# A state-space scan and a low-rank mixer on one core: half a batch moved from plain to split products, and a new order

## The chip, the cores and the metric

The kernel runs on one core of a Trainium2 chip. A core has a matrix engine (PE, with PEld for its weight loads), a vector engine (DVE), a scalar engine (ACT), a general engine (POOL) and a queue engine (SP) that issues the DMAs. The metric is the time in microseconds on the device, from the start to the end of one execution; less is better.

## The reference

Two parts follow each other. The first is a scan over 768 positions for 4 batches and 8 heads (head size 32, state size 16), the second a mixer over the 256 channels that the heads make together.

```python
# scan, by chunks of 32 positions
L = np.exp(cum[:, :, :, None] - cum[:, :, None, :]) * causal
y_intra = ((Cc @ Bc^T) * L) @ xc
y_inter = (Cc @ state) * exp(cum)
state   = decay_full * state + sum(Bc x xc * decay_from_j)
# mixer on x = y laid out as (batch, position, 256)
h  = x^T @ U @ V                              # rank 32, along positions
u  = x + h^T
ch = np.maximum(u @ w_ch1, 0.0) @ w_ch2       # 256 -> 1024 -> 256
return u + ch
```

The weights U, V, w_ch1 and w_ch2 come as 64-bit floating point numbers and are turned into 32-bit ones on the core.

## The kernel before, in words

**An order written out by hand.** The whole program is a list of words, `PLAN`. The function `follow` reads it from left to right, and every word issues a small group of instructions. Each engine works off its own instructions in the order in which the words issued them, and waits for the data of the others. So the list sets the order on every engine, and a word that has to wait on one engine holds up what stands behind it on that engine alone.

**Loads**, all on SP's queue: `B k`, `X k` and `w n` bring the scan's B and C, its x, and a block of the weights. `k` counts pairs of 128-position chunks, 0 to 11, three for each batch. These loads are also held until the last DVE instruction issued before them is done. `YB`, `YX`, `YU` and `YV` are the same loads for B and C, x, U and V, without that hold. `YV` issues four DMAs of 48 KB, `YU` one of 192 KB, `YX` two of 128 KB, `YB` three.

**Weights.** `c n` appears three times for each block: the first time two DVE instructions and one of ACT, the second time one of DVE, the third time one of POOL. Block 0 is U and V together, so its first word needs the loads of both. Blocks 1 to 5 are the first layer, 6 to 9 the second. `R n` (two or three times) splits a weight block into halves of 12 bits for the one-pass products: an ACT copy, then a POOL subtraction and another ACT copy, then one DVE instruction. `v` spreads V over the partitions.

**Scan**, for pair k: `Q`, `P` scale B and C by decays (DVE); `V`, `T` turn them with PE and copy the result on ACT (and for some `V` on DVE); `g` forms the products of C and B (PE), `m` and `M` mask them (DVE), `s` the sums for the state (PE), `u` updates the state (DVE, then POOL), `i`, `n` and `j` make the output (PE; `j` waits for a small settling copy on DVE), and `y` copies it (ACT). `A` and `K` at the start make the decays. `t` and `O` turn the output back for the mixer.

**Mixer**, for batch b: `p`, `q` and `a` do the low-rank part (`a b.j` adds it to half j of the positions, 384 of them, on DVE). Then the two layers, for each half j. In the plain form a word `U b.j.m` makes one block of 128 hidden channels from 32-bit operands (two products) and a ReLU on ACT, and `d b.j.k.n`, n from 0 to 3, the second layer for 128 positions. In the split form `S b.j` first cuts u into a near part, a far part and a sum (one ACT instruction, two of DVE); for each block m, `f` makes four of six one-pass products and a scaling on ACT, `e` the last two and a ReLU on ACT, `h` the far part on DVE and, for odd m, the sum as well; `d b.j.k.n`, n from 0 to 5, is the second layer. The choice is in `down`:

```python
parts = b or j >= PLAIN
pieces = 6 if parts else 4
```

With `PLAIN = 2` both halves of batch 0 are plain, and the other three batches split.

**Buffers and fills.** Products go to eight banks of the accumulator memory, two under each of the tags w, x, z and y; a word that takes a bank waits until the last reader of that bank's earlier content is done. The tag `words` has 15 buffers for the weights' words, their temporaries, and the hidden channels. `F n` makes the next word that takes a bank run n idle blocks of 128 columns on PE ahead of its own products (line 136); `E n` runs n such blocks at once.

The lines that the profile names: L136 idle blocks, L202 the loads, L174 every DVE instruction (a helper issues them), L425 the last step of `c`, L439 the subtraction of `R`, L478 `V` and `T`, L510 `g`, L545 `s`, L630 `i`, L655 `n` and `j`, L682 `t` and `O`, L709 and L717 `p`, L727 `q`, L737 `a` and the closing product, L765 all products of the two layers, L858 `v`.

Of the kernel before, what the change touches and what calls it, by code (L numbers as in the profile page):

```python
# [13 lines left out]
FP32R = mybir.dt.float32r  # L14
WCOLS = 512
NWORDS = 15
PLAIN = 2
TAGS = {(2, 1): "yyy", (3, 0): "yyy", (3, 1): "yyy"}


# [11 lines left out]


PLAN = (
    'YB0 F2 A1 YB1 Q0.2 A0 Q0.0 Q0.1 YX0 K0 YB2 YV0 F5 V0.0.0 V0.1.1 F1 g0 Q1.2 Q1.1 s0 V1.1.2 YX1 '
    'Q1.0 V1.0.2 m0 M0 n0 YX2 F3 g1 Q2.0 Q2.2 u0 YU0 M1 Q2.1 i0 j0 y0 s1 F1 V2.0.2 m1 n1 w0 u1 '
    'V2.1.3 c0 c0 c0 E3 i1 g2 m2 YB3 w1 M2 E4 j1 y1 s2 B5 v0 O0.0 w4 u2 c2 t1 i2 P3 X3 c2 B4 w2 c2 '
    'n2 j2 T3 c1 c1 y2 T3 O2.1 X4 p0 P5 g3 m3 M3 q0 T5 T5 n3 a0.1 a0.0 B6 c1 s3 U0.1.0 P4 w3 U0.1.1 '
    'u3 T4 T4 U0.0.1 i3 c5 c5 c3 g4 X5 j3 c5 c3 w5 s4 U0.0.0 m4 R3 U0.1.6 c3 y3 U0.1.2 P6 U0.0.6 M4 '
    'T6 u4 T6 B7 i4 g5 c4 c4 n4 w6 s5 j4 y4 R1 M5 U0.0.7 c4 U0.1.3 m5 U0.1.7 U0.0.5 R3 c6 u5 U0.0.3 '  # L40
    'P7 T7 w8 n5 R0 i5 c7 R2 X6 c6 g6 w7 j5 c6 y5 T7 U0.1.5 t5 M6 U0.0.2 X9 B10 c7 t3 m6 R2 t4 R1 '
    'c8 U0.0.4 c8 p1 U0.1.4 c7 B8 q1 R4 X7 c8 d0.0.2.0 c9 d0.0.1.0 c9 d0.0.1.1 c9 d0.0.2.1 d0.0.2.2 '
    'd0.0.2.3 d0.1.0.0 a1.0 d0.1.0.1 P8 d0.1.0.2 S1.0 a1.1 R7 d0.0.1.2 d0.0.1.3 d0.1.0.3 s6 g7 m7 '
    'M7 n6 R0 f1.0.0 u6 R6 f1.0.1 f1.0.4 e1.0.0 h1.0.0 f1.0.5 e1.0.4 e1.0.1 f1.0.6 h1.0.4 i6 s7 j6 '
    'h1.0.1 d0.0.0.0 e1.0.5 R4 h1.0.5 f1.0.7 X8 e1.0.6 h1.0.6 d0.0.0.1 d0.0.0.2 e1.0.7 h1.0.7 '
    'f1.0.3 R5 f1.0.2 B9 u7 d0.1.1.0 X10 d0.0.0.3 P10 e1.0.2 R5 y6 h1.0.2 S1.1 e1.0.3 d0.1.2.0 '
    'd0.1.1.1 d0.1.1.2 h1.0.3 d0.1.2.1 d0.1.2.2 T8 T8 d0.1.2.3 d0.1.1.3 n7 s8 u8 i7 g8 j7 P9 s9 '
    'f1.1.0 m8 y7 R7 f1.1.1 d1.0.1.0 M8 e1.1.0 u9 d1.0.0.0 i8 n8 h1.1.0 s10 j8 d1.0.1.1 d1.0.1.2 R6 '
    'd1.0.1.3 R4 R5 u10 d1.0.0.1 d1.0.0.2 d1.0.1.4 e1.1.1 d1.0.0.3 R7 d1.0.2.0 R6 d1.0.2.1 d1.0.2.2 '
    'B11 d1.0.2.3 d1.0.0.4 d1.0.0.5 d1.0.1.5 d1.0.2.4 T10 h1.1.1 f1.1.6 f1.1.7 d1.0.2.5 e1.1.6 '  # L50
    'e1.1.7 f1.1.2 h1.1.6 h1.1.7 f1.1.3 f1.1.4 f1.1.5 X11 e1.1.2 e1.1.4 h1.1.2 h1.1.4 e1.1.3 h1.1.3 '
    'e1.1.5 P11 h1.1.5 T9 T9 d1.1.0.0 d1.1.0.1 d1.1.2.0 d1.1.2.1 d1.1.0.2 d1.1.2.2 d1.1.0.3 y8 t6 '
    'd1.1.2.3 d1.1.1.0 d1.1.1.1 d1.1.1.2 d1.1.1.3 d1.1.2.4 d1.1.0.4 d1.1.0.5 t7 d1.1.1.4 d1.1.1.5 '
    'd1.1.2.5 T10 t8 g9 p2 m9 M9 i9 g10 m10 q2 T11 T11 M10 n9 a2.0 s11 u11 j9 g11 i10 n10 y9 m11 '
    'S2.0 M11 t9 f2.0.0 f2.0.4 f2.0.1 e2.0.0 h2.0.0 e2.0.4 f2.0.5 e2.0.1 h2.0.4 h2.0.1 f2.0.6 '
    'e2.0.5 h2.0.5 f2.0.2 f2.0.3 j10 y10 e2.0.2 e2.0.3 f2.0.7 h2.0.2 h2.0.3 i11 n11 a2.1 e2.0.6 '
    'e2.0.7 j11 h2.0.6 d2.0.0.0 S2.1 y11 d2.0.1.0 d2.0.1.1 d2.0.0.1 f2.1.0 h2.0.7 d2.0.1.2 t11 t10 '
    'e2.1.0 h2.1.0 d2.0.1.3 d2.0.0.2 d2.0.0.3 f2.1.2 d2.0.1.4 d2.0.0.4 d2.0.0.5 d2.0.1.5 f2.1.3 '
    'd2.0.2.0 e2.1.2 h2.1.2 e2.1.3 d2.0.2.1 p3 d2.0.2.2 f2.1.1 f2.1.4 h2.1.3 d2.0.2.3 e2.1.1 f2.1.5 '
    'h2.1.1 e2.1.4 h2.1.4 d2.0.2.4 e2.1.5 q3 d2.0.2.5 h2.1.5 f2.1.6 f2.1.7 a3.0 e2.1.6 e2.1.7 '  # L60
    'h2.1.6 d2.1.2.0 d2.1.2.1 a3.1 d2.1.0.0 d2.1.0.1 d2.1.2.2 d2.1.0.2 S3.0 f3.0.3 f3.0.2 h2.1.7 '
    'd2.1.2.3 d2.1.0.3 f3.0.1 e3.0.2 h3.0.2 d2.1.0.4 e3.0.3 d2.1.0.5 h3.0.3 f3.0.0 e3.0.1 d2.1.1.0 '
    'd2.1.1.1 d2.1.1.2 e3.0.0 h3.0.0 f3.0.5 f3.0.4 d2.1.1.3 f3.0.6 e3.0.4 d2.1.2.4 e3.0.5 h3.0.1 '
    'f3.0.7 h3.0.4 d2.1.2.5 d2.1.1.4 e3.0.6 e3.0.7 d2.1.1.5 d3.0.2.0 d3.0.2.1 h3.0.6 d3.0.2.2 '
    'd3.0.0.0 d3.0.0.1 d3.0.0.2 S3.1 f3.1.0 f3.1.4 f3.1.5 h3.0.7 h3.0.5 d3.0.2.3 e3.1.0 f3.1.1 '
    'h3.1.0 d3.0.0.3 e3.1.4 f3.1.2 e3.1.5 d3.0.0.4 d3.0.0.5 d3.0.2.4 d3.0.2.5 d3.0.1.0 h3.1.4 '
    'd3.0.1.1 h3.1.5 e3.1.1 f3.1.6 f3.1.3 h3.1.1 d3.0.1.2 e3.1.2 e3.1.3 d3.0.1.3 h3.1.2 h3.1.3 '
    'f3.1.7 e3.1.6 h3.1.6 d3.0.1.4 d3.0.1.5 e3.1.7 d3.1.2.0 d3.1.2.1 h3.1.7 d3.1.2.2 d3.1.2.3 '
    'd3.1.1.0 d3.1.1.1 d3.1.2.4 d3.1.2.5 d3.1.1.2 d3.1.1.3 d3.1.0.0 d3.1.0.1 d3.1.0.2 d3.1.0.3 '
    'd3.1.1.4 d3.1.1.5 d3.1.0.4 d3.1.0.5 ')  # L70


@with_exitstack
def kernel(
# [624 lines left out]
    def mixer(b):  # L699
# [110 lines left out]
        def down(j, k, n):  # L810

            parts = b or j >= PLAIN
            pieces = 6 if parts else 4
# [141 lines left out]
```

## Time and profile before

| | |
|---|---|
| median of 3 runs | 227.23 us (226.65 to 227.78) |
| the profiled execution | 225.44 us, of which the span of instructions is 223.7 us |
| PE busy | 214.8 us, 96% of the span |
| DVE, ACT, POOL busy | 146.7, 107.9 and 33.8 us |
| granted PE clock | 0.999 |
| DMA | 14.59 MB, queue busy 32.3% of the span, nearly all before 70 us |
| chain that ended last | PE 88%, SP's queue 5%, DVE 3% |

Times in the rows are microseconds from the start of the span. A product's duration in a row is how long that one was under way; products overlap, so what a step costs is read from the chain of work or from where the next one starts. A plain product of 32-bit operands shows as two records.

### The profile page before, as it was taken

The numbers are of one execution on the slowest core, as the hardware profiler recorded it, in microseconds if no ns is written. First come the engines' busy times: TensorE is split into PE (matmuls) and PEld (weight loads), VectorE is DVE, ScalarE is ACT, GpSimd is POOL, SyncE is SP. The second block draws the span as 40 slices with busy tenths as digits, with TensorE's granted clock in tenths as the row PEclk, the third lists the DMA queues.
The fourth block names the chain that finished last, engine by engine and source line by source line (L and its number), as shares of the span: only waits on it lengthen the run. The fifth ranks groups of instructions, "written<-read, shape, count | busy, mean of one in ns | idle before, by whom it ended". The sixth has DMA issues, their size and how long they took to land.

```text
span 223.7 us, 7032 instructions
## 1 busy us (share of the span) xinstructions
PE 214.8 (96%) x3024; PEld 182.1 (81%) x3024; DVE 146.7 (66%) x311; ACT 107.9 (48%) x250; POOL 33.8 (15%) x43
## 2 busy tenths in 40 slices
PE   7878999999999999999999999999999999999994
PEld 4645655666668888887999997797999999999993
DVE  4867779927853866759636737978825966484821
ACT  3334746575781354461425624577336555554510
POOL 3012301642834020223400000000000000000000
PEclk9999999999999999999999999999999999999999
DMA  6968889962973010461032301000010000101011
GB/s 81 142 105 151 172 134 175 231 139 84 196 97 52 26 50 0 61 107 50 7 47 70 50 22 53 3 3 3 0 50 0 25 3 23 38 8 50 1 50 47
DMA packets 69520, 14.59 MB, mean 65 GB/s; under 512 B 63792, under 2 KB 67696, under 8 KB 69488
## 3 DMA queue, kind: packets, MB, share of 16 engines
q1 hardware_dynamic: 69488, 14.13, 32.3%
q8 instruction: 24, 0.39, 0.8%
q14 instruction: 8, 0.07, 0.1%
HBM read 10.98 MB, written 3.15 MB: 63 GB/s over the span
## 4 chain that ended last, share of the span: by engine, by line
PE 88%; SPq 5%; DVE 3%; DMA 1%; issue 1%; ACT 1%
PE x L765 31%; PE z L765 23%; PE y L765 12%; SPq L202 5%; PE y L655 3%; PE y L630 3%; PE w L682 2%; PE x L510 2%; PE w L545 2%; DMA x<-in_x_dram 1%; PE w L478 1%; DVE M L174 1%; PE z L510 1%; PE w L709 1%; PE x L737 1%; PE w L136 1%
## 5 line engine op out<-in xcount | busy, mean ns | idle before, releaser
L765 PE MATMUL x<-u,w 128*128 128x384 f32 x144 | 32.8, 344 | 0.2 <-DVE M L174 0.2
L765 PE MATMUL z<-u,w 128*128 128x384 f32 x144 | 32.6, 342 | 0.0
L174 DVE SCALAR_TENSOR_TENSOR words<-words 128x768 fp32r<-128x768 f32 (+3 forms) x34 | 30.1, 887 | 1.6
L770 ACT ACTIVATE x<-x 128x384 f32<-128x384 f32 (+1 forms) x30 | 13.6, 454 | 28.4 <-PE x L765 28.4
L765 PEld LDWEIGHTS z<-u,w 128*128 128x128 f32 x144 | 24.9, 188 | 0.6 <-DVE M L174 0.2
L765 PEld LDWEIGHTS x<-u,w 128*128 128x128 f32 x144 | 24.4, 188 | 1.0 <-issue 0.3
L765 PE MATMUL x<-w2c,words 128*128 128x256 f32 x112 | 22.9, 341 | 0.0
L174 DVE SCALAR_TENSOR_TENSOR words<-x,words 128x384 fp32r<-128x384 f32 x24 | 13.1, 554 | 14.8 <-ACT words L799 12.9
L572 POOL TENSOR_TENSOR Sm<-S,own 128x256 f32<-128x256 f32 (+1 forms) x12 | 8.1, 676 | 84.9 <-DVE S L174 47.5
L765 PEld LDWEIGHTS x<-w2c,words 128*128 128x128 f32 x112 | 18.2, 189 | 1.6
L765 PE MATMUL y<-w,words 128*128 128x256 f32 x144 | 19.3, 282 | 0.0
L770 ACT ACTIVATE z<-z 128x384 f32<-128x384 f32 (+1 forms) x27 | 12.5, 465 | 13.0 <-PE z L765 12.6
L765 PEld LDWEIGHTS y<-w,words 128*128 128x128 f32 x144 | 18.7, 190 | 0.0
L174 DVE SCALAR_TENSOR_TENSOR words<-z,words 128x384 fp32r<-128x384 f32 x24 | 13.2, 551 | 5.4 <-ACT words L799 5.4
L799 ACT ACTIVATE words<-z 128x384 fp32r<-128x384 f32 x24 | 11.7, 492 | 9.9 <-PE z L765 9.7
L799 ACT ACTIVATE words<-x 128x384 fp32r<-128x384 f32 x24 | 11.6, 491 | 7.8 <-PE x L765 7.8
L765 PE MATMUL x<-w,words 128*128 128x256 f32 x96 | 13.8, 286 | 0.0
L174 DVE SCALAR_TENSOR_TENSOR S<-S,kept,w 128x64 f32<-128x64 f32 x40 | 11.2, 279 | 2.8 <-PE w L545 1.2
L174 DVE TENSOR_TENSOR ytok<-x,ytok 128x256 f32<-128x256 f32 x10 | 4.2, 423 | 13.2 <-PE x L765 13.2
L655 PE MATMUL y<-M,x 64*32 64x64 f32 x768 | 12.0, 223 | 0.9 <-DVE settled L174 0.9
L765 PEld LDWEIGHTS x<-w,words 128*128 128x128 f32 x96 | 12.5, 190 | 0.3 <-issue 0.2
L655 PEld LDWEIGHTS y<-M,x 64*32 64x32 f32 x768 | 7.8, 105 | 5.8 <-DVE settled L174 1.9
(150 smaller groups left out, 409.7 us busy)
## 6 DMA issues: line engine op xcount, KB each, us to landing
words<-in_moe_w_ch_dram SPq DMA_DIRECT2D x7, 512.0 KB, 4.9
x<-in_x_dram SPq DMA_DIRECT2D x24, 128.0 KB, 3.5
out_dram<-ytok SPq DMA_DIRECT2D x24, 128.0 KB, 1.7
bc<-in_B_dram SPq DMA_DIRECT2D x24, 64.0 KB, 2.9
bc<-in_C_dram SPq DMA_DIRECT2D x12, 128.0 KB, 3.1
words<-in_moe_w_ch_dram SPq DMA_DIRECT2D x2, 256.0 KB, 3.8
words<-in_moe_V_dram SPq DMA_DIRECT2D x4, 48.0 KB, 3.4
words<-in_moe_U_dram SPq DMA_DIRECT2D x1, 192.0 KB, 3.4
```

The costliest lines, as they stand in the source:

```text
L136: nc.tensor.matmul(out=t[:, :m * P].rearrange("p (m i) -> p m i", i=P), lhsT=ident, rhs=ident[:, None, :].to_broadcast([P, m, P]), start=T ...
L174: self.last = call(*args, **kwargs)
L202: op = issuer[0].dma_start(**kwargs)
L510: nc.tensor.matmul(out=g[r][cols, c], lhsT=s["T"][rows, 0, c, cols], rhs=s["Cm"][rows, :, :, ts(2 * c + p, Q)].rearrange("r v t i -> r v i ...
L545: nc.tensor.matmul(out=s["A"][p][ts(r, Q), v], lhsT=s["BC"][half, 0, v, 2 * r:2 * r + 2].rearrange("p h n -> p (h n)"), rhs=x_sb[k][half, ...
L572: nc.gpsimd.tensor_tensor(out=s["Sm"][:, sl], in0=s["S"][:, sl].rearrange("p i (s d) -> p i s d", s=2), in1=own2[:, b, 4 * q + sl.start:4 ...
L630: behind["first"].append(nc.tensor.matmul(out=y[r // 2][ts(r % 2, H), c, p], lhsT=own[ts(r, Q)], rhs=s["T"][ts(r, Q), 1, :, ts(2 * c + p, ...
L655: product = nc.tensor.matmul(out=y[n][ts(i, Q), c, p], lhsT=x_sb[k][half, c, h], rhs=s["M"][half, h // 2, c, h % 2], start=fresh(k, n, [i] ...
L682: nc.tensor.transpose(out=t[:, c, g], in_=yT[b][:, g, ts(2 * q + c, P)], identity=ident)
L765: nc.tensor.matmul(out=t, lhsT=lhsT, rhs=rhs, start=start, stop=True, skip_group_check=True)
L770: nc.scalar.activation(t, t, AF.Copy, scale=1.0 + EPS)
L799: nc.scalar.activation(gs[j, m // 2][0][:, m % 2], t, AF.Relu, scale=NEAR)
```

## The change

`PLAIN` becomes 1: the first half of batch 0 stays plain, the second half takes the split form. The eight words `U0.1.m` go; `S0.1`, eight each of `f0.1.m`, `e0.1.m` and `h0.1.m`, and six more words `d0.1.k.n` come. The whole list stands in a new order. The words `F` are placed anew (6, 5, 4, 3 and 4 blocks in place of 2, 5, 1, 3 and 1), and the two words `E3` and `E4` go. No function changes. The two lists as far as the second layer of batch 0 (from batch 2 on they are much alike):

```diff
@@ -14,7 +14,7 @@
 FP32R = mybir.dt.float32r
 WCOLS = 512
 NWORDS = 15
-PLAIN = 2
+PLAIN = 1
 TAGS = {(2, 1): "yyy", (3, 0): "yyy", (3, 1): "yyy"}
...
 PLAN = (
-    'YB0 F2 A1 YB1 Q0.2 A0 Q0.0 Q0.1 YX0 K0 YB2 YV0 F5 V0.0.0 V0.1.1 F1 g0 Q1.2 Q1.1 s0 V1.1.2 YX1 '
-    'Q1.0 V1.0.2 m0 M0 n0 YX2 F3 g1 Q2.0 Q2.2 u0 YU0 M1 Q2.1 i0 j0 y0 s1 F1 V2.0.2 m1 n1 w0 u1 '
-    'V2.1.3 c0 c0 c0 E3 i1 g2 m2 YB3 w1 M2 E4 j1 y1 s2 B5 v0 O0.0 w4 u2 c2 t1 i2 P3 X3 c2 B4 w2 c2 '
-    'n2 j2 T3 c1 c1 y2 T3 O2.1 X4 p0 P5 g3 m3 M3 q0 T5 T5 n3 a0.1 a0.0 B6 c1 s3 U0.1.0 P4 w3 U0.1.1 '
-    'u3 T4 T4 U0.0.1 i3 c5 c5 c3 g4 X5 j3 c5 c3 w5 s4 U0.0.0 m4 R3 U0.1.6 c3 y3 U0.1.2 P6 U0.0.6 M4 '
-    'T6 u4 T6 B7 i4 g5 c4 c4 n4 w6 s5 j4 y4 R1 M5 U0.0.7 c4 U0.1.3 m5 U0.1.7 U0.0.5 R3 c6 u5 U0.0.3 '
-    'P7 T7 w8 n5 R0 i5 c7 R2 X6 c6 g6 w7 j5 c6 y5 T7 U0.1.5 t5 M6 U0.0.2 X9 B10 c7 t3 m6 R2 t4 R1 '
-    'c8 U0.0.4 c8 p1 U0.1.4 c7 B8 q1 R4 X7 c8 d0.0.2.0 c9 d0.0.1.0 c9 d0.0.1.1 c9 d0.0.2.1 d0.0.2.2 '
-    'd0.0.2.3 d0.1.0.0 a1.0 d0.1.0.1 P8 d0.1.0.2 S1.0 a1.1 R7 d0.0.1.2 d0.0.1.3 d0.1.0.3 s6 g7 m7 '
-    'M7 n6 R0 f1.0.0 u6 R6 f1.0.1 f1.0.4 e1.0.0 h1.0.0 f1.0.5 e1.0.4 e1.0.1 f1.0.6 h1.0.4 i6 s7 j6 '
-    'h1.0.1 d0.0.0.0 e1.0.5 R4 h1.0.5 f1.0.7 X8 e1.0.6 h1.0.6 d0.0.0.1 d0.0.0.2 e1.0.7 h1.0.7 '
-    'f1.0.3 R5 f1.0.2 B9 u7 d0.1.1.0 X10 d0.0.0.3 P10 e1.0.2 R5 y6 h1.0.2 S1.1 e1.0.3 d0.1.2.0 '
-    'd0.1.1.1 d0.1.1.2 h1.0.3 d0.1.2.1 d0.1.2.2 T8 T8 d0.1.2.3 d0.1.1.3 n7 s8 u8 i7 g8 j7 P9 s9 '
...
+    'F6 A1 YB1 YB0 A0 Q0.0 YX0 Q1.2 Q0.2 Q0.1 V0.0.0 YX1 YU0 V0.1.1 YB2 K0 YV0 w2 Q1.0 F5 g0 s0 YX2 '
+    'u0 Q1.1 s1 m0 M0 YB3 V1.0.2 F4 V1.1.2 c0 c0 n0 Q2.2 i0 g1 j0 y0 F3 w1 Q2.0 B5 Q2.1 V2.0.2 u1 '
+    'm1 M1 c3 O0.0 s2 c3 V2.1.3 i1 w3 n1 j1 u2 c0 y1 g2 w0 c3 X3 B4 P3 T3 m2 w4 c2 i2 T3 w7 t1 M2 '
+    'n2 j2 P5 y2 T5 w8 c4 X4 O2.1 T5 p0 c4 g3 M3 m3 q0 w6 F4 c4 X5 v0 P4 c1 s3 n3 u3 R2 a0.0 a0.1 '
+    'T4 T4 c5 U0.0.2 U0.0.3 i3 c8 c2 c1 g4 j3 s4 y3 U0.0.4 m4 M4 c8 c2 B6 c9 U0.0.1 c5 c1 R0 c5 '
+    'U0.0.0 n4 u4 c7 c8 w5 s5 i4 g5 u5 j4 B10 y4 P6 B7 T6 T6 U0.0.7 M5 m5 n5 R0 c9 i5 t3 j5 c9 X7 '
+    'y5 c6 c6 R1 c6 U0.0.6 t5 t4 R3 X6 c7 c7 g6 p1 M6 m6 P7 U0.0.5 R4 q1 d0.0.2.0 d0.0.2.1 B8 T7 R1 '
+    'R5 a1.0 R3 R7 T7 S0.1 X8 d0.0.1.0 d0.0.1.1 d0.0.2.2 d0.0.2.3 R2 d0.0.1.2 n6 R4 s6 u6 R6 '
+    'd0.0.1.3 s7 g7 m7 R6 i6 B9 f0.1.2 f0.1.0 M7 f0.1.1 e0.1.2 h0.1.2 e0.1.0 h0.1.0 f0.1.3 P8 '
+    'e0.1.1 f0.1.4 R5 d0.0.0.0 h0.1.1 e0.1.3 e0.1.4 h0.1.4 R7 f0.1.5 d0.0.0.1 X10 d0.0.0.2 h0.1.3 '
+    'u7 f0.1.6 d0.0.0.3 R7 R6 e0.1.5 h0.1.5 f0.1.7 j6 s8 e0.1.7 e0.1.6 d0.1.1.0 R5 d0.1.0.0 '
+    'd0.1.0.1 d0.1.1.1 d0.1.1.2 d0.1.2.0 h0.1.6 d0.1.2.1 y6 d0.1.0.2 h0.1.7 d0.1.0.3 u8 R4 d0.1.1.3 '
+    'd0.1.2.2 d0.1.2.3 d0.1.0.4 d0.1.0.5 S1.0 T8 P9 X9 d0.1.2.4 d0.1.1.4 d0.1.2.5 d0.1.1.5 f1.0.6 '
...
```

## The prediction

> **What bounds the kernel now.** I read the busy time of the engines by stretch first.
>
> ```profile
> 0.00:25.00 25.00, 20.75 (x490) 13.36 (x490) 16.58 (x57) 10.21 (x31) 5.17 (x17) 1.00 0.78 123
> 25.00:50.00 25.00, 24.59 (x516) 15.60 (x509) 18.69 (x47) 15.30 (x37) 8.04 (x8) 1.00 0.87 175
> 50.00:75.00 25.00, 24.81 (x233) 17.77 (x232) 15.84 (x30) 14.55 (x32) 10.96 (x9) 1.00 0.54 102
> 200.00:224.00 24.00, 20.51 (x157) 20.25 (x155) 10.30 (x18) 7.78 (x19) 0.00 (x0) 0.98 0.10 34
> ```
>
> Columns: stretch, length, busy us of PE, PEld, DVE, ACT, POOL, granted clock, DMA share, GB/s. PE is full from 25 on. Only the first 25 us (which hold idle blocks as well) and the tail have room. So the end is the moment at which the unbroken PE work begins, plus the work then left. Next, the chain that ended last (start, us, what, records), for the prices:
>
> ```profile
> 40.02 5.36 PE x L765 x16
> 68.79 3.57 PE x L765 x17
> 122.98 0.70 PE x L765 x4
> 193.60 3.46 PE y L765 x29
> ```
>
> First row: four steps U0 (plain products, four records each), 1.34 us a step. Second: one 128-row group of the plain second layer, 16 records and a closing one: 3.57. Third: one step f, 0.70, or 0.175 a record; step e has two records, 0.35. Fourth: 0.119 a record of the one-pass second layer, so 25 records (24 and a closing one) take 2.98. Last, the order of time in the front:
>
> ```profile
> 9.10 1.98 SPq L202 DMA_DIRECT2D words<-in_moe_V_dram  x4
> 18.96 0.63 DVE L174 TENSOR_SCALAR words<-words 128x384 f32<-128x384 f32 x2 [0.30 <-DMA words<-in_moe_U_dram]
> 27.68 1.54 PE L709 MATMUL w<-ytok,UV 128*32 128x256 f32 x12
> 33.21 1.56 PE L765 MATMUL x<-yT,w1f 128*128 128x384 f32 x4
> ```
>
> V's four loads are issued at 9.10 to 11.08. The first conversion (c0, which needs U and V both) starts the moment that U has landed. p0 is at 27.68. The first large product, U0.1.0, is at 33.21: there the dense work begins, and 223.7 - 33.2 = 190.5 us follow.
>
> **PE work removed.** Eight steps U0.1 at 1.34 become f and e at 1.05: 2.3 less. Three groups d0.1 go from 3.57 to 2.98: 1.8 less. Together 4.1. On a full engine this counts whole, wherever it stands.
>
> **DVE and ACT work added.** DVE: split 2 x 0.957, eight h at 0.553, four joins at 0.958: 10.2 us. ACT: 0.85, eight scalings at 0.476, three at 0.37: 5.8 us. Both stand behind f0.1, where PE has some 20 us of f, e and d, so I cost them at nothing: from f0.1.2 to the last d0.1 the list holds 22 us of PE beside 17 to 19.5 of DVE (with and without the 0.08 by which neighbours overlap), and in the old list's like stretch, 75 to 110, DVE had 24.9 of 35 and PE lost 0.4. If that cover failed, the price is at most the 4.4 of the eight h. The twelve words buffers that they take are free, since every c word stands ahead of f0.1.
>
> **Fills.** 19 blocks of 128 columns become 22. The chain's "18.01 0.66 PE w L136 x2" is the three blocks of E3: 0.22 us a block. They cost only where PE was not going to wait.
>
> **The front, which is reordered.** The likely end hangs on when U0.0.2, the new first large product, can start. I walk there with durations of the rows. (a) Six fills ahead of A1, from 3.6 on, let A1 start at 4.9, not 4.74; ACT's second F ends near 6.45, the four BC pieces at 7.7, V0.0.0 and V0.1.1 at 8.05. In SP's queue YB0 now stands behind YB1, and at that place loads landed in time. (b) K0 occupies PE to 8.9, then five fills to 10.0. g0 could have begun near 9.3 (T of V0.1.1), so F5 costs 0.7. g0 ends 10.7, s0 11.2. u0 now stands ahead of the masks on DVE: 12.5, then Q1.1, m0 and M0: 14.2, where M0 ended at 11.38 before. (c) Next on DVE is c0. V's loads now stand behind YX1 (two of 128 KB) and YU0 (192 KB) on SP. Before, the last was issued at 10.67 and 3.4 us is its median to landing: 14.1. Three issues more at 0.63 make 16.0; 448 KB at the 144 GB/s of 7.5 to 10 us make 17.2; the queue was half idle at 10 to 15 us (share 0.66 and 0.53), so nothing at all is the lower bound. I take 16.3, near the issue bound, since issue set the pace there. DVE waits 2.1 us. Behind c0 on DVE are Q2.2, the settling copy that j0 waits for, Q2.0, Q2.1, u1, m1 and M1. (d) So j0 is at 17.9 (14.84 before), u1 ends 19.7, M1 21.1. V2.0.2 needs the x bank that m1 frees, and runs at 20.7 with its three fills inside that wait; ACT's three copies end 22.2; V2.1.3 22.5, i1 23.2, j1 24.4 (20.95 before), g2 25.1. (e) m2, c2, M2 to 27.8; n2, j2, y2, O2.1 at 0.5 to 0.8 each, and two ytok copies on DVE: p0 at 31.4 (27.68 before). (f) v0, which ran at 22.5 before, now follows q0. From the end of g3 at 33.2 DVE has no pause: masks 1.4, ps 0.4, UV 0.4, P4 0.7, c1 0.6, u3 1.3, a0.0 1.0, in all 5.8. U0.0.2 starts at 39.1.
>
> **The sum.** By U0.0.2 the new list has done the same scans as the old one had by U0.1.0, and two T4 words (0.6) more; the order of batches 2 and 3 is nearly the old one, and I cost its changes at nothing, as PE waited for next to nothing in any such order before. Left are 190.5 - 4.1 - 0.6 = 185.8 us. 39.1 + 185.8 = 224.9. Break-even is a start at 37.9.
>
> Two terms lie behind U0.0.2. On SP's queue w7 and w8 (512 KB each) now pass X4: at the 175 GB/s of 25 to 50 that is 6 us, from 36 (issued at 32.55, median 3.5) to 42; s4, which needs it, comes at 44: nothing, with 0 to 2 as bounds. And from 39 to 61 DVE has 16 to 18.6 us of words (a0.1 to c7's second step) beside 22 of PE, and i4 comes due at 49 just as u4 ends. POOL's conversions lie there too, and DVE suffers beside POOL:
>
> ```profile
> 50.43 0.69 DVE L174 SCALAR_TENSOR_TENSOR w<-words,w 128x512 fp32r<-128x512 f32 x1 [1.36 <-POOL words L439]
> 59.77 2.79 DVE L174 SCALAR_TENSOR_TENSOR w<-words,w 128x512 fp32r<-128x512 f32 x2
> 57.36 2.95 POOL L439 TENSOR_TENSOR words<-w1f,w 128x512 f32<-128x512 f32 x2 [0.74 <-ACT w L435]
> 60.27 1.74 POOL L425 TENSOR_TENSOR w2c<-words 128x512 int32<-128x512 int32 x1
> ```
>
> The same instruction (the last of an R step) takes 0.69 with POOL idle, and two of them 2.79 with POOL busy from 57.36 to 62.01: 0.7 more for each. I take 0.5 of PE idle, between 0 and 3.5 (five such meetings, none of them hidden).
>
> [...]
>
> Span 225.4, against 223.7: 1.7 more. The profiled execution took 225.44, 1.74 of it around the span; so 227.1. The median of the three runs is 227.23, 1.8 above the profiled one; I add the same difference to it: 229.0.
>
> **The rivals.** Half a percent (1.1 us) is about what a measurement of this kernel can tell from no change.
>
> *V has landed when c0 comes up.* For it: the half idle queue at 10 to 15 us. Against: SP's pace of 0.6 us an issue, and landing 2 to 4 us behind. The chain from (c) on moves by 1.9, U0.0.2 to 37.2, the end to 223.5 with the 0.5: 227.0, the same.
>
> *The front keeps its pace* and the whole saving lands. For it: until 25 us PE has 4.2 us idle besides its fills, DVE 8.4, so an order that uses them can take up the c words for nothing; SP could also deliver U and V at 15, ahead of DVE. Against: v0, u0 and c0 each stand ahead of work that the old list had first. U0.0.2 would start between 34 and 36, with the 0.5 a time of 223.8 to 225.8.
>
> *DVE becomes the bound between 39 and 61.* For it: the 2.79 above and i4 without slack. Against: PE waited for DVE there before only 0.4 us in all. It decides once POOL stops DVE by more than the 3 us between c6's end (58) and d0.0.2.0 (61), or u4 by any amount. Price 2 to 3.5 more: 231 to 232.5.
>
> **How the numbers follow.** Forecast (slower by 1.2 to 3.3 us: its own range 228.4 to 230.5) 0.45; V in time 0.17; front keeps pace 0.25; DVE bound 0.13. Hence faster 0.25, same 0.17, slower 0.58. Low end of the range: 224.4, which leaves out the lower part of the second rival (0.1); high end 231.8, which leaves out the upper part of the third (0.07).
>
> **What would show it.** Right: in the first 25 us c0's first DVE instruction waits for words of V or U near 14 to 16; the p0 row (L709) near 31; the first x<-yT,w1f row near 39; PE's total for L765 falls by some 4; from 40 on PE over 24.5 of each 25. The first rival shows c0 without a DMA wait and the first product at 37; the second, at 36 or earlier; the third, PE waits on DVE at L630, L655 and L765 between 45 and 62 that total over 2 us. I am wrong in the mechanism if the first large product starts late and the end still comes early, because PE idle after 40 was larger before than I read it.

## The result, and the profile after

The kernel after the change takes 233.53 us (median of 6 runs, 232.61 to 234.62), the one before 226.65 us (6 runs, 225.78 to 227.78). The ratio is 1.030, with a 95% interval of 1.0255 to 1.0349: slower by 3%, where 0.8% was forecast. The profiled execution after took 234.62 us, the longest of the six, and its span is 232.9 us; that of before (225.44, span 223.7) was shorter than any of its six. So the two profiles differ by 9.2 us where the medians differ by 6.9. In three runs below (new_front_old_rest, front_light3, front_dve3) the profiled execution was a disturbed one, with rows that are used only to say where an engine stood, and the times given for these three and for new_order_plain leave out their disturbed executions. Lines of the changed kernel are numbered 2 higher than before, those of the other kernels 1 to 3.

First the busy time by stretch, with the columns that the prediction explains:

```profile
0.00:25.00 25.00, 19.75 (x312) 12.00 (x316) 14.06 (x49) 8.66 (x23) 3.62 (x15) 0.93 0.79 131
25.00:50.00 25.00, 22.45 (x528) 13.94 (x517) 21.00 (x57) 14.45 (x36) 7.97 (x9) 1.00 0.80 174
50.00:75.00 25.00, 23.82 (x518) 18.06 (x518) 19.55 (x40) 15.79 (x34) 16.36 (x14) 1.00 0.60 99
75.00:100.00 25.00, 22.82 (x193) 21.86 (x192) 15.04 (x31) 10.94 (x25) 3.50 (x4) 0.93 0.19 33
200.00:232.90 32.90, 29.68 (x220) 29.15 (x218) 17.47 (x29) 12.40 (x28) 0.00 (x0) 1.00 0.10 33
```

PE is no longer full from 25 us on: it lacks 2.6 us in the second stretch and 2.2 in the fourth. And the granted clock, which was full in nearly all of before, is 0.93 in the first stretch and in the fourth. Next the order of time in the front, first PE and then SP's queue and DVE (start, length, what, records, and in brackets the idle time ahead of it and what ended it):

```profile
3.77 2.77 PE L138 MATMUL w<-ident 128*128 128x512 f32 x4
...
20.01 0.48 PE L512 MATMUL z<-Cm,T 32*64 32x128 f32 x4 [1.51 <-issue]
...
33.63 1.32 PE L711 MATMUL w<-ytok,UV 128*32 128x256 f32 x12
...
41.01 1.53 PE L767 MATMUL x<-yT,w1f 128*128 128x384 f32 x4
```

```profile
11.76 1.97 SPq L204 DMA_DIRECT2D words<-in_moe_V_dram  x4
...
15.89 0.62 DVE L176 TENSOR_SCALAR words<-words 128x384 f32<-128x384 f32 x2
```

The six idle blocks ahead of A1 took 2.77 us, 0.46 a block and not 0.22. V's loads went out by 13.73, and c0 (last row) began without a wait. PE stood for 1.51 us in the middle of g1, with no releaser that the profile knows. The first large product came at 41.01.

The other new loss lies at 86 us. PE's rows, then DVE's, then the stretches of two microseconds:

```profile
88.32 0.46 PE L657 MATMUL y<-M,x 64*32 64x64 f32 x32 [2.19 <-DVE settled L176]
88.58 0.53 PE L547 MATMUL w<-x,BC 64*32 64x64 f32 x24
89.04 0.87 PE L767 MATMUL z<-u,w 128*128 128x384 f32 x2
```

```profile
85.11 0.42 DVE L176 TENSOR_TENSOR ytok<-x,ytok 128x256 f32<-128x256 f32 x1 [0.37 <-PE x L767]
85.46 1.28 DVE L176 SCALAR_TENSOR_TENSOR w2c<-w,w 128x512 fp32r<-128x512 f32 x2
86.66 0.55 DVE L176 SCALAR_TENSOR_TENSOR words<-z,words 128x384 fp32r<-128x384 f32 x1
87.24 0.96 DVE L176 SCALAR_TENSOR_TENSOR words<-words 128x768 fp32r<-128x768 f32 x1
88.12 0.14 DVE L176 COPY settled<-slot 128x1 f32<-128x1 f32 x1
```

```profile
86.00:88.00 2.00, 0.13 (x1) 0.00 (x0) 1.97 (x4) 0.47 (x1) 0.00 (x0) 1.00 0.19 66
88.00:90.00 2.00, 1.68 (x59) 1.59 (x60) 0.86 (x3) 0.05 (x1) 0.00 (x0) 0.80 0.00 0
90.00:92.00 2.00, 2.00 (x10) 2.00 (x10) 0.89 (x2) 1.47 (x4) 0.00 (x0) 0.50 0.00 0
```

j6 waits for the settling copy, which DVE reaches only behind the last steps of R7 and R6 and behind h0.1.5. R7 and R6 write buffers that the plain second layer still reads, and on DVE they stand behind the closing copy of d0.0.0 (first row), which waits for its last product (85.1). PE stands for 2.19 us, and then works for 3.41 us at half clock (89.22 to 92.63 in the clock's records).

**Where the 9.2 us of the two spans lie.** PE idle time, added up from its records in order of start, is 10.5 us against 4.3: 6.2 more. Full clock began at 7.30 instead of 4.63: at most 1.3. Two windows of 3.41 us at half clock, from 20.95 and from 89.22: at most 1.7 each (estimates, half of each length, as an idle block took 0.46 us ahead of 7.30 and 0.22 at full clock). Three fill blocks more: 0.7. Products: 2.6 less (worked out below, from a run without the second window). Together 9.0 at most. Cut at the first large product, 7.8 of the 9.2 us lie ahead of it (41.0 against 33.2) and 1.4 behind it (191.9 us against 190.5, where the prediction had 186.3).

### The profile page after: what moved, and what is told of

Its sections match the earlier page's. It is cut to its first block, busy times and chain, and to the rows that moved or that the text cites. A ratio compares the mean times of both kernels' runs of the same rounds, so it can differ in the third digit from the quotient of the medians.

```text
span 232.9 us, 7133 instructions
## 1 busy us (share of the span) xinstructions
PE 217.8 (93%) x3062; PEld 187.2 (80%) x3062; DVE 154.6 (66%) x325; ACT 113.7 (49%) x262; POOL 33.2 (14%) x43
## 3 DMA queue, kind: packets, MB, share of 16 engines
q1 hardware_dynamic: 69488, 14.13, 30.9%
HBM read 10.98 MB, written 3.15 MB: 61 GB/s over the span
## 4 chain that ended last, share of the span: by engine, by line
PE 89%; DVE 6%; issue 2%; ACT 1%; POOL 0%; POOLq 0%; DVEq 0%
PE x L767 30%; PE z L767 22%; PE y L767 12%; PE y L657 4%; PE y L632 2%; PE w L547 2%; PE x L512 2%; PE x L138 2%; PE w L480 2%; PE w L684 2%; DVE words L176 2%; DVE M L176 1%; PE z L512 1%; DVE BC L176 1%; PE w L138 1%
## 5 line engine op out<-in xcount | busy, mean ns | idle before, releaser
L767 PE MATMUL x<-u,w 128*128 128x384 f32 x168 | 38.9, 349 | 0.2 <-DVE M L176 0.2
L767 PE MATMUL z<-u,w 128*128 128x384 f32 x168 | 38.1, 345 | 0.0
L772 ACT ACTIVATE x<-x 128x384 f32<-128x384 f32 (+1 forms) x36 | 16.4, 455 | 28.8 <-PE x L767 27.1
L767 PEld LDWEIGHTS x<-u,w 128*128 128x128 f32 x168 | 28.6, 190 | 1.9 <-ACT x L772 0.4
L767 PEld LDWEIGHTS z<-u,w 128*128 128x128 f32 x168 | 29.0, 188 | 0.9 <-ACT words L801 0.2
L767 PE MATMUL x<-w,words 128*128 128x256 f32 x128 | 18.1, 291 | 0.0
L767 PE MATMUL x<-w2c,words 128*128 128x256 f32 x96 | 17.8, 317 | 0.0
L767 PEld LDWEIGHTS x<-w,words 128*128 128x128 f32 x128 | 17.0, 199 | 0.1
L767 PEld LDWEIGHTS x<-w2c,words 128*128 128x128 f32 x96 | 14.9, 189 | 0.7
L512 PE MATMUL z<-Cm,T 32*64 32x128 f32 x192 | 10.8, 306 | 1.5 <-issue 1.5
```

Of the source, the lines that this page charges most:

```text
L512: nc.tensor.matmul(out=g[r][cols, c], lhsT=s["T"][rows, 0, c, cols], rhs=s["Cm"][rows, :, :, ts(2 * c + p, Q)].rearrange("r v t i -> r v i ...
L767: nc.tensor.matmul(out=t, lhsT=lhsT, rhs=rhs, start=start, stop=True, skip_group_check=True)
L772: nc.scalar.activation(t, t, AF.Copy, scale=1.0 + EPS)
```

## The experiments

Medians are in us; each kernel ran beside the kernel before on the same chip, and each ratio is to that, with its 95% interval.

**The wait of j6.** In `j6_early` the word j6 stands ahead of f0.1.1 and no longer behind R7, R6 and h0.1.5.

```diff
- ... B9 f0.1.2 f0.1.0 M7 f0.1.1 ... R7 R6 e0.1.5 h0.1.5 f0.1.7 j6 s8 ...
+ ... B9 f0.1.2 f0.1.0 M7 j6 f0.1.1 ... R7 R6 e0.1.5 h0.1.5 f0.1.7 s8 ...
```

> The changed kernel with one word moved: j6 goes from behind f0.1.7 to ahead of f0.1.1, so that its settling copy on DVE stands ahead of P8, the h words and the R7 and R6 words and not behind them. Theory 1 (the loss lies in where words were put): the 2.2 us wait of PE at 86 goes, and with it the 3.4 us of half clock behind it, which cost 1.7: 3.9 less than the changed kernel's 233.5, so about 229.6, and no half clock near 89 in the trace. Rival (the split form's added DVE and ACT work is what costs, 10.2 and 5.8 us): the wait moves to e0.1.6, h0.1.6 or the first d0.1, and less than 1 us is gained.

231.51 (230.58 to 232.38), ratio 1.0203 (1.0128 to 1.0278), some 2 us less than after. The wait is gone, and so is the half clock behind it: the span is 230.4, PE idle 9.0 us. From the first large product to the end it takes 189.0 us where after took 191.9, so the wait and the half clock cost 2.9 together. That stretch repeats well: first_fill_2 below, which has after's list there, takes 191.8. All kernels below that say so are built on this one.

`fill_at_j6` leaves the wait where it is and puts nine idle blocks on PE ahead of it.

```diff
- ... f0.1.7 j6 s8 ...
+ ... f0.1.7 E9 j6 s8 ...
```

> The list of after, unchanged but for nine idle blocks (2.0 us at full clock) on PE right ahead of j6, which waits 2.19 us for DVE there. The wait stays; only PE is busy in it. Theory 'the 3.4 us at half clock that follow come from PE standing still, and cost 1.7 us by themselves': the half clock near 89 is gone and the time falls by 1.0 to 1.7, to 231.8 to 232.5 us. Rival 'the clock costs nothing because the work behind waits for DVE and ACT anyway': 233.2 to 234 us, as after.

231.30 (230.99 to 233.14), ratio 1.0259 (1.0212 to 1.0305): 2.2 less than after by the medians, 1.0 by the ratios, whose intervals overlap. The same three stretches in this kernel:

```profile
86.00:88.00 2.00, 1.77 (x63) 1.69 (x64) 0.77 (x3) 0.40 (x2) 0.00 (x0) 1.00 0.00 0
88.00:90.00 2.00, 2.00 (x19) 2.00 (x18) 1.46 (x3) 1.01 (x4) 0.00 (x0) 1.00 0.03 8
90.00:92.00 2.00, 2.00 (x19) 2.00 (x18) 1.87 (x5) 0.00 (x0) 0.52 (x1) 1.00 0.00 0
```

The clock stays full, though DVE is no earlier; DVE's copy still ends the last 0.25 us of the wait. So the half clock came from PE standing still, and it has a price of its own: from the first large product on this kernel takes 190.4 us, 1.5 less than after. What else its profile gained (2.1 us) lies ahead of the first large product, where its list is that of after; more on that below.

**The front and the split form, each alone.** `old_front` keeps before's order and fills ahead of the split half, leaves out U0.1 and puts S0.1 behind the R words that it needs; `old_front2` mends what that run showed. `new_order_plain` is the new list with plain steps U0.1 in the places of f0.1. `new_front_old_rest` is the new list up to the first large product, and before's list from there on, all plain.

```diff
  old_front2, against old_front:
- ... c1 s3 P4 w3 u3 ... U0.0.1 ... s6 g7 m7 n6 R0 S0.1 u6 R6 ...
+ ... c1 s3 U0.0.0 P4 w3 U0.0.1 u3 ... s6 u6 g7 m7 n6 R0 S0.1 R6 ...   (and j6 early)
```

> Split form of the second half as in the changed kernel, and its list from f0.1.2 on; everything ahead of f0.1.2 stands in the order of the kernel before, with its fills (F2 F5 F1 F3 F1 E3 E4), without the words U0.1; S0.1 behind the last of R0 to R3. Theory 1: the first large product comes near 33 as before and not at 41; some of the gained 8 us is lost again, since without U0.1 (10.7 us) PE runs dry beside the weights' conversion between 35 and 60; the end gains 3 to 5 us, so 228.5 to 230.5, the wait at j6 still in it. Rival (added work costs, the front does not matter): within 1 us of 233.5.

> The new list with PLAIN 2: U0.1.m stands where f0.1.m stood, S0.1, e0.1 and h0.1 are gone, d0.1 has four plain pieces, and the last words of R4 to R7 stand behind the last d0.1, since they overwrite the plain weights. PE work is 4.1 us more than in the changed kernel, DVE work 10.2 and ACT work 5.8 less. Theory 1 (placing): the front is as late as in the changed kernel; the wait at j6 and its half clock go, because h0.1.5 and the R words no longer stand ahead of it (3.9 less); 233.5 + 4.1 - 3.9 = 233.7. Rival (added work): back to the 227 of before.

> The mirror image: the front of before, and the split half behind it as in after with j6 early. Against old_front (237.9 us) the eight steps U0.0 stand where the first of each pair of steps stood, u6 directly behind s6 and no longer behind R0 and S0.1 on DVE, so that the waits of 2.65 and 4.71 us are gone. If the split form needs only those two repairs: 227.5 to 230 us. Rival 'with eight plain steps fewer PE runs dry while weights are converted and split, wherever the eight stand': PE idle over 8 us between 33 and 75, with half clock behind it, 233 us or more.

> No split in batch 0 here: all sixteen plain steps stay, and behind the first large product the list of before is kept. Only what stands ahead of the first large product is in the new order, with its fills and loads. So it shows what the new front costs by itself. By the profiles of before and after the first large product comes 7.8 us later, and up to five words of weights (1.8 us of DVE) are left over for later. Theory 'the front is the cost, the split saves 2 to 4': slower than before by 5 to 8 us, 231 to 234. Rival 'the front is late only because work was moved into it, which is missing later': 227 to 229.5.

237.9 (ratio 1.0496, 1.0439 to 1.0552), 237.93 (1.0512, 1.0434 to 1.0589), 238.02 (1.0534, 1.0493 to 1.0575) and 238.78 (1.0605, 1.0551 to 1.0659). Three miss both of their expectations; old_front2 has the time that its rival gave. All four are slower than the whole change. Each makes a large wait of its own (old_front, new_order_plain, new_front_old_rest):

```profile
77.94 0.92 PE L633 MATMUL y<-T,Sm 32*64 32x64 f32 x24 [4.71 <-POOL Sm L575]
```

```profile
103.68 0.62 PE L766 MATMUL x<-u,w 128*128 128x384 f32 x2 [3.22 <-DVE u L175]
```

```profile
45.66 1.01 PE L766 MATMUL x<-yT,w1f 128*128 128x384 f32 x1 [4.22 <-POOL w1f L426]
```

In the last, the new front has converted other weight blocks than those that the old rest asks for first. old_front2 has no wait over 1.6 us, but many small ones. Here is PE (second number) between 33 and 75 us, in before and then in old_front2:

```profile
33.00:75.00 42.00, 41.81 (x577) 28.78 (x564) 28.64 (x62) 24.71 (x54) 17.52 (x14) 1.00 0.67 136
```

```profile
33.00:75.00 42.00, 35.76 (x683) 24.59 (x690) 29.45 (x68) 20.81 (x44) 17.55 (x15) 0.96 0.64 131
```

PE stands for 6.2 of the 42 us where it stood for 0.2: without the eight plain steps U0.1 it runs dry while the weights are converted, as the rival had it (with over 8 us). So these runs do not divide the 7 us into a cost of the front and a cost of the split: each alone costs 12 to 13, and together they cost 7. The split form needs an order of its own, and the new front pays only with it.

**The start of the front.** `first_fill_2` puts two idle blocks ahead of A1 in place of six (`F6` becomes `F2`).

> The changed kernel with F2 in place of F6 as its first word. In the trace of the changed kernel the six idle blocks ran at half clock and took 2.8 us, and A1 came at 6.47 and not 4.74. Theory 1a (that start is on the path): four blocks at half clock go, 1.7 us less: 231.8. Rival: the loads and the DVE words behind them set the pace, or the clock's rise is pushed back by the idle time: less than 0.6 us.

234.54 (233.59 to 236.8), ratio 1.036 (1.0281 to 1.0439): no gain. M0 ends 1.5 us earlier (14.52), but then DVE stands 2.67 us for V, which is the wait that the prediction had forecast for the change itself. Behind it j0 waits 1.53 us for DVE and V2.0.2 1.42, and the clock is half from 19.78 to 36.84.

**DVE's order in the front.** On j6_early, `front_dve` puts the masks ahead of u0, the first two words c0 behind M1, the first c2 behind M2, and s1 behind V1.1.2.

```diff
- ... g0 s0 YX2 u0 Q1.1 s1 m0 M0 YB3 V1.0.2 F4 V1.1.2 c0 c0 n0 ... m1 M1 c3 ... m2 w4 c2 i2 T3 w7 t1 M2 n2 ...
+ ... g0 s0 YX2 Q1.1 m0 M0 u0 YB3 V1.0.2 F4 V1.1.2 s1 n0 ... m1 M1 c0 c0 c3 ... m2 w4 i2 T3 w7 t1 M2 c2 n2 ...
```

> The list with j6 early, and DVE's order in the front set as in the list before: the masks m0 M0 ahead of u0, the two c0 words behind M1 and not ahead of the settling of j0, the first c2 behind M2; s1 behind V1.1.2, so that it does not wait for its bank. Theory 'the words of c0, u0 and c2 ahead of the scan's masks cost the front 2 to 3 us': M0 ends near 14.7 instead of 16, the 0.9 us wait of n2 and the 1.1 us hold in s1 go, 228.5 to 230 us. Rival 'held by PE's instructions and the low clock, whatever DVE does': the hold in g1 and the half clock stay, under 0.7 us gained, 230.8 to 231.6 us.

230.35 (229.59 to 230.68), ratio 1.0189 (1.0154 to 1.0225): the fastest of all these kernels, 1.2 below j6_early by the medians, though their intervals overlap. The waits in s1 (1.13) and n2 (0.92) are gone, but the hold in g1 grew to 2.95 us and took most of it back:

```profile
17.09 0.30 PE L513 MATMUL z<-Cm,T 32*64 32x128 f32 x1
20.34 0.48 PE L513 MATMUL z<-Cm,T 32*64 32x128 f32 x3 [2.95 <-issue]
```

**The loads.** `w2_late` is j6_early with w2 moved behind w1, `front_both` is front_dve with the same.

> The list with j6 early (231.5 us), and the 512 KB load w2 moved behind w1, so that V, X2 and B3 no longer stand beside it. In the trace of after, SP stood 3.76 us at B3's first issue, an instruction packet of 16 KB came only at 17.73, and PE stood 1.51 us in the middle of g1; the granted clock of the window after that was 0.5. Theory 'PE's instructions arrive late behind the loads': the packet comes by 15, the hold in g1 falls under 0.4 us, the half clock at 21 goes or moves, 228 to 230 us. Rival 'DVE sets the pace there': the hold turns into a wait for DVE of the same size, 231 to 232 us. A third way: c2's first step finds its words late (issue after 21), 232 to 233 us.

> Both edits at once (w2 behind w1; masks ahead of u0, c0 behind M1, c2 behind M2, s1 behind V1.1.2), with j6 early. If late instructions and DVE's order are each worth 1.5 to 2.5 us and add up: 226.5 to 228.5 us, as before within a per cent, PE idle near 6 us instead of 9. If one hides the other: no better than the better one of the two runs ahead of it.

231.59 (1.0257, 1.0227 to 1.0287) and 231.68 (1.0261, 1.0218 to 1.0304): no gain, and front_both is 1.3 us slower than front_dve by the medians, with intervals that just overlap. I had taken c2 for the reader of w2; it is c3, whose words now came late (in w2_late j1 waits 2.84 us for DVE). The hold in g1 fell to 0.54 in w2_late and stayed at 2.33 in front_both.

The hold has one feature in common: in every run that has it, PE stands behind exactly 449 of its recorded instructions (products, weight loads and waits), and goes on 2.2 to 3.3 us after the start of a packet of 16,384 bytes on an instruction queue. That PE stands there for its instructions is inferred from these times; no record names what it waits for. Four more runs were to find out why the packet is late. `before_loads` is the kernel of before with X1 and U ahead of B2 and V and w2 behind V; `front_loads` is front_dve with before's order of loads, `front_loads_f2` the same with `F2`.

```diff
  before_loads:
- ... YX0 K0 YB2 YV0 F5 ... V1.1.2 YX1 ... u0 YU0 M1 ... B4 w2 c2 ...
+ ... YX0 K0 YX1 YU0 YB2 YV0 w2 F5 ... V1.1.2 ... u0 M1 ... B4 c2 ...
  front_loads:
- ... YX0 ... YX1 YU0 V0.1.1 YB2 K0 YV0 w2 Q1.0 F5 g0 s0 YX2 ... YB3 ... g1 j0 ... w1
+ ... YX0 ... V0.1.1 YB2 K0 YV0 Q1.0 F5 g0 s0 YX1 ... V1.1.2 YX2 ... g1 YU0 YB3 j0 ... w1 w2
```

> The kernel of before with nothing changed but its loads: X1 and U moved ahead of B2 and V, and w2 right behind V, as in the new list. Theory 'the early loads hold up PE's instructions': the first packet comes at 13 to 17 instead of 10.98, PE stands 0.5 to 3 us behind its 449th instruction, 227.5 to 230.5 us. Rival 'the loads' order costs nothing, it is the new order of PE's and DVE's own work': the packet comes near 11, 225.5 to 226.8 us.

> The list with j6 early and DVE's front order as before (front_dve, 230.35 us), and now the loads on SP's queue in the order of the list before too: B1, B0, X0, B2, V, X1, X2, U, B3, w1, w2. In every run of the new order the hold inside g1 stands at the same place, behind 449 instructions of PE, and ends 2.2 to 2.5 us after the start of an instruction packet of 16 KB (17.73, 18.04, 16.67, 18.13, 16.95, 17.16); in the runs whose packet came at 14.05 and 14.53 there was no hold, and before had its packet at 10.98. Theory 'the early loads hold the packet up': it comes by 13, no hold in g1 and no half clock at 21, 2.9 + 1.7 us less: 225.5 to 227. Rival 'the packet is late by something else of the new order': it comes at 16 to 18 and the hold stays, 229.5 to 231. A mishap on the way: c0 or s1 waits for U or X1, up to 1.5 us.

> The same with two idle blocks ahead of A1 in place of six. In the profile of after the six ran at half clock and A1 came at 6.47 instead of 4.74, so the front could begin 1.7 us sooner. Theory 'the start is on the path once nothing holds the front': 1.0 to 1.7 less than front_loads, 224 to 226. Rival 'as in the run of the list of after with two blocks, the front then waits for DMA and the clock drops': no gain or up to 1.5 more.

before_loads: 229.9 (228.33 to 230.59), ratio 1.0164 (1.0117 to 1.0211). The order of the loads alone costs the old list 3.9 us, but not by the packet, which came at 12.65. PE's row, and DVE's, which it waits for by way of u0:

```profile
17.16 0.82 PE L631 MATMUL y<-T,Sm 32*64 32x64 f32 x24 [2.56 <-POOL Sm L573]
```

```profile
14.71 0.42 DVE L175 TENSOR_TENSOR BC<-bc,F 128x256 f32<-128x256 f32 x1 [1.88 <-DMA bc<-in_C_dram]
```

B2's part for C, now behind X1 and U, lands at 14.69 instead of 10.82; PE is idle for 1.4 us more in all than before, and the clock is half from 17.34 to 24.16, which is worth up to 3.4 (half of the 6.82 us). front_loads: 232.64 (1.0282, 1.0235 to 1.0329), front_loads_f2: 232.84 (1.0281, 1.0227 to 1.0335). With before's order of loads the packet of front_loads still came at 16.69, so that order is not enough to bring it early. c3 waited again (j1 1.89 and 2.28 us), and in front_loads_f2 s1 waited 1.89 for X1.

`front_light` and `front_light2` take load off the DMA engines ahead of the packet: X2, U and V are held until Q1.1 (front_light) or M0 (front_light2), B3 until u0. front_light has w2 late once more, front_light2 has it behind V; front_light_f2 is front_light with `F2`.

```diff
  front_light2, against front_dve:
- ... YX1 YU0 V0.1.1 YB2 K0 YV0 w2 Q1.0 F5 g0 s0 YX2 Q1.1 m0 M0 u0 YB3 V1.0.2 ...
+ ... YX1 V0.1.1 YB2 K0 Q1.0 F5 g0 s0 Q1.1 m0 M0 X2 YU0 YV0 w2 u0 B3 V1.0.2 ...
```

> front_dve (230.35 us) with its loads spread out: X2 held until DVE has scaled B for pair 1 (near 12.6 us), U and V behind X2, B3 held until u0, w2 behind w1; X1 stays early. So little is queued on the DMA engines when PE comes to its 205th instruction (near 13 us), where the packet of before came (10.98, at PE's 209th). Theory 'the packet waits its turn among the queued loads': it comes by 14.5, there is no hold behind the 449th instruction, and with it goes the half clock at 21: 225.5 to 227.5 us. Rival 'the packet comes 3.6 to 5 us behind the 200th instruction of the new order whatever is queued': the hold of 1.8 to 3 us stays, 229.5 to 231 us.

> The same with two idle blocks ahead of A1 in place of six: PE and the front begin up to 1.7 us sooner, and X1 is early, so that s1 does not wait for it as it did in front_loads_f2 (1.89 us). Theory 'the front is then bound by its own work': 0.7 to 1.7 less than front_light. Rival 'the loads or the clock (half after thin windows) take it back': 0 to 1.5 more.

> front_light (232.9 us) had a fault of its own: c3 reads the load w2, which was moved behind w1, and DVE stood 4.67 us for it (j1 then waited 3.3, and the clock was half for 6.8 us). Here w2 goes behind V again, and X2, U and V are held until the masks M0 are done (near 13 us), B3 until u0, so that nothing is queued when PE comes to its 205th instruction near 12 to 13 us. front_light's packet came at 15.07, 3 us behind PE's 200th instruction, with a hold of 1.56. Theory 'the packet waits behind queued loads': it comes within 1.5 us of the 200th instruction, no hold behind the 449th, 226.5 to 228.5 us. Rival 'late by the order of PE's own work': 3 us or more behind it and a hold of 1.5 to 3 us, 229.5 to 231 us.

232.89 (1.0301, 1.028 to 1.0321), 233.01 (1.0297, 1.0273 to 1.032) and 231.95 (1.0254, 1.0191 to 1.0317). front_light and front_light_f2 were spoiled by c3, which stood 4.67 and 5.32 us for w2. front_light2 had its packet at 13.89 and no hold, as the theory had it, but lost that by DVE waiting for the loads that now come later (c0, then c3), with j1 2.94 us late behind it and 6.8 us of half clock:

```profile
20.66 0.63 DVE L177 TENSOR_SCALAR words<-words 128x384 f32<-128x384 f32 x2 [0.97 <-DMA words<-in_moe_V_dram]
...
23.21 0.76 DVE L177 TENSOR_SCALAR words<-words 128x512 f32<-128x512 f32 x2 [1.34 <-DMA words<-in_moe_w_ch_dram]
```

Two last runs put c0 behind M2 and c3 behind P5, with the loads of front_light2 (`front_light3`) and with those of front_dve (`front_dve3`).

```diff
- ... m1 M1 c0 c0 c3 O0.0 s2 c3 V2.1.3 ... u2 c0 y1 g2 w0 c3 X3 ... M2 c2 n2 j2 P5 y2 T5 w8 c4 X4 O2.1 T5 ...
+ ... m1 M1 O0.0 s2 V2.1.3 ... u2 y1 g2 w0 X3 ... M2 c0 c0 c2 n2 j2 c0 P5 y2 T5 c3 c3 w8 c4 X4 O2.1 c3 T5 ...
```

> front_light2 (231.95 us) had its packet at 13.89, 0.9 us behind PE's 200th instruction, and no hold, but c0 and c3 then stood 0.97 and 1.34 us on DVE for V and w2, which land later there, and held up the settling of j1 (PE idle 2.94 us, then 6.8 us at half clock). Here the words c0 go behind M2 and c3 behind P5, where their loads have long landed. If the front now has neither wait: 2.9 us of idle and most of 3.4 us of half clock less, 226 to 228 us, as before or 1 per cent above. Rival 'the weights' words then come late for the first large product': PE waits for w1f or POOL's third steps near 39, up to 3 us, 228.5 to 231.

> The same places of c0 and c3, but the loads early as in the list of after (X1, U, B2, V, w2, X2, B3 one behind the other). So it differs from front_light3 only in what is queued on the DMA engines when PE's second packet of instructions falls due. Theory 'the queued loads hold the packet up, and that is what the hold and the half clock at 21 cost': packet at 16 to 18, hold 1.5 to 3 us, 1.5 to 4 us slower than front_light3. Rival 'the hold only takes the place of waits that come anyway': within 1 us of it.

232.3 (230.98 to 234.37; 1.0267, 1.0219 to 1.0314) and 232.49 (232.0 to 234.98; 1.03, 1.0243 to 1.0357). The difference of 0.2 (0.7 by the ratios) is what the rival forecast (within 1 us) and not the 1.5 to 4 of the theory; as the intervals overlap, a price of the early loads is not shown, and neither kernel gained. And front_light3 speaks against the theory itself: with the loads of front_light2, and the DMA engines without a data packet from 13 to 15 us, its instruction packet came at 16.29. The table has all that bears on it (us; "200th" is the time at which PE has 200 recorded instructions behind it):

| kernel | 200th | packet | PE stood behind its 449th |
|---|---|---|---|
| before | 10.14 | 10.98 | 0 |
| old_front, old_front2 | 10.55, 11.10 | 11.50, 11.84 | 0 |
| before_loads | 11.24 | 12.65 | 0 |
| after | 12.88 | 17.73 | 1.51 |
| j6_early | 12.94 | 18.04 | 1.83 |
| fill_at_j6 | 11.95 | 14.53 | 0 |
| first_fill_2 | 12.78 | 14.05 | 0 |
| new_order_plain | 12.53 | 17.16 | 1.53 |
| w2_late | 12.89 | 16.67 | 0.54 |
| front_dve, front_both | 13.21, 12.77 | 18.13, 16.95 | 2.95, 2.33 |
| front_loads, front_loads_f2 | 13.06, 11.93 | 16.69, 12.78 | 1.83, 0 |
| front_light, front_light_f2 | 12.04, 13.69 | 15.07, 14.37 | 1.56, 0 |
| front_light2 | 12.96 | 13.89 | 0 |
| front_light3, front_dve3 | 13.03, 12.83 | 16.29, 18.40 | 2.38, 3.69 |

The packet follows the 200th instruction by 0.7 to 5.6 us, and the hold appears whenever it comes after 15. What decides its time stays open: neither the order of the loads (front_loads) nor what is queued (front_light3) explains it alone. Nor does the list: after, j6_early and fill_at_j6 have the same words up to the first large product, and their packets came at 17.73, 18.04 and 14.53. With one profile of each kernel, no packet's time can be put down to an edit. No version beat the kernel before.

## Why the prediction was right or wrong

The direction was right, and in outline the mechanism (a late front that more than eats the saved products). The size was not: 225.4 was forecast for the span and 232.9 found. Ahead of the first large product 1.9 us were missing in the sum, behind it 5.6 (186.3 forecast, 191.9 found). By the steps of the prediction:

- **(a), (b): a front walked at full clock.** A1 came at 6.47, not 4.9: the six fills ahead of it took 0.46 us each, where the walk had 0.22, and the first record of full clock begins at 7.30. M0 ended at 15.98, not 14.2. How early the clock rises differs from run to run (full from 4.63 in the profile of before, from 4.7 to 7.5 in the others). On DVE this was made up by the next step: M1 ended at 21.23, where 21.1 was forecast.
- **(c): V lands at 16.3 and DVE waits 2.1 us.** Wrong. SP issued V by 13.73, it landed at 15.22, and c0 began at 15.89 with no wait. The first rival had that point right, but its time was not reached. On PE, j0 came at 20.4, where 17.9 was forecast: in g1, ahead of it, PE stood 1.5 us behind its 449th instruction, and then worked 3.4 us at half clock. The walk has no term for either. In fill_at_j6, with the same words, PE did not stand there, M0 ended 0.9 us earlier than in after, and j0 and the first product came 2.6 and 2.1 earlier, within 0.2 of the forecast (17.9 and 39.1):

```profile
17.86 0.45 PE L658 MATMUL y<-M,x 64*32 64x64 f32 x32
...
38.91 0.88 PE L768 MATMUL x<-yT,w1f 128*128 128x384 f32 x2
```

- **(d) to (f).** M2 ended at 30.9, where 27.8 was forecast. Part of it is c2: (e) left no room for POOL there, but its first two instructions ran beside two conversions of POOL and took 2.2 us, where the same two took 0.5 later with POOL idle (first and last row, of after). So what the prediction priced for 39 to 61 us struck in the front; no run tests it alone. From M2 to p0 it went 0.9 faster than forecast; p0 came at 33.6 (31.4), the first product 7.4 behind p0 (7.7 forecast), v0 late as described. That fill_at_j6 met the forecast was in part luck: V in time and c2 beside POOL cancel.

```profile
28.05 2.20 DVE L176 TENSOR_SCALAR words<-words 128x256 f32<-128x256 f32 x2
27.80 1.01 POOL L427 TENSOR_TENSOR UV<-words 128x384 int32<-128x384 int32 x1
28.76 1.33 POOL L427 TENSOR_TENSOR w1f<-words 128x512 int32<-128x512 int32 x1
38.58 0.49 DVE L176 TENSOR_SCALAR words<-words 128x256 f32<-128x256 f32 x2
```

- **PE work removed, 4.1 us.** The term was mis-sized: 2.6. In j6_early, PE's time for the layers, each overlap counted once, changes by -10.75 for U (as forecast), -1.72 for d (1.8 forecast) and +9.88 for f and e, where 8 x 1.05 = 8.4 was taken. The new half took 9.2 us, and the seven halves together 61.8 where six had taken 51.9. The 1.05 was the step back to back; in lists that alternate f, e, d and scans it was 1.08 on average before and 1.15 in the new half. What makes it longer there is not shown.
- **DVE and ACT work "at nothing".** This step failed outright. The cover of 22 us of PE was there, but the order on DVE decided: R7 and R6, behind a copy that waits for the last product of d0.0.0, and h0.1.5 stood ahead of j6's settling copy. Price: 2.19 us of wait and up to 1.7 of half clock; moving j6 alone took 2.9 off this stretch. The prediction gave 4.4 as the price if the cover failed, but for the h steps, and put none of it into the sum.
- **The rest of the order, 0.5 us between 39 and 61.** About right: 0.29 and 0.68, the larger behind ACT and not DVE. The third rival, which had DVE as the bound there at 231 to 232.5, came near in size by another mechanism, 25 us later.

The forecast of 225.4, with 1.9 at the front, 2.9 at j6, 1.5 for f and e and 0.5 more of waits between 39 and 61, gives 232.2 of the 232.9 found; the last 0.7 stays open. What the prediction named as its sign of being right (PE over 24.5 of each 25 from 40 on) was not there: 23.8 and 22.8.

The clock was left out altogether. All clock records here, but for the last of each run, are 3.41 us long or a multiple of it, and in after it fell to half behind two windows of 3.41 us with PE busy for 55% (17.54 to 20.95) and 36% (85.81 to 89.22). The three stretches found here are worth up to 4.7 us (1.3, 1.7 and 1.7 by the estimates above).

## What to carry to other kernels

Where one engine is nearly full, price each place at which it may stand not by the wait alone but by the wait and the half clock that can follow it (2.19 us and 3.41 us at j6 in after); filling a wait with idle work can win back a good part of what removing it does (1.5 of 2.9 us here). Work that is covered in sum can still be on the path through its order: look at what stands ahead of each small copy that the full engine waits for, and at which buffer's last reader holds that up. An order and a form of the work that were tuned together do not come apart: taking either half alone cost more than both.

## What the runs showed that was not expected

**The clock fell behind windows that were half empty, even without one long gap.** In 20 profiles, every one of the 31 windows of 3.41 us at full clock that was followed by half clock (the end of each run left out) had PE busy for 59% of it or less, with single gaps from 0.76 us up; none with 60% or more was. It is no sharp bound: five windows between 49 and 55% stayed full. At half clock the share did not decide: in first_fill_2 the clock stayed half behind windows with PE busy 72, 98, 93 and 90%, 17.1 us in all, and in front_loads_f2 it rose behind one with 91%.

**PE's hold follows a packet of instructions.** In 20 profiles PE never passed its 449th recorded instruction sooner than 2.2 us after the first 16 KB packet of instructions had started, and that packet started anywhere from 10.98 to 18.40 us. That PE waits for this packet is inferred from the two times; no record names it. The profile calls this wait "issue", as it does with what reads as a wait for a bank (s1 at 13.1, 1.13 us: it goes on 0.1 us after the third state update of u0, and with s1 moved behind u0 in front_dve the wait is gone).
